# Seven products for w_in: partial sums that accumulate in PSUM, and four additions that also take the row maximum

## The chip, the core and the metric

The kernel runs on one core of a Trainium2 chip. The core has a matrix engine (TensorE, PE in the profile, with its weight loads as PEld), a vector engine (DVE), a scalar engine (ACT), GpSimd (POOL) and a queue engine (SP) that here only issues transfers. Each engine takes its own instructions strictly in the order in which they were written, and engines wait for one another by semaphores. PE's results go to banks of PSUM, which DVE and ACT read; the other tiles lie in SBUF. The metric is the device time of one execution in microseconds, as the median of several runs.

## The reference

```python
q_n, k_n = rmsnorm(q, g_q), rmsnorm(k, g_k)            # q, k, v: (8, 12, 448, 64)
scores = q_n @ k_n.T / sqrt(64)
attn = softmax(scores);  o = attn @ v
x = o.transpose(0, 2, 1, 3).reshape(3584, 768)
h = x @ w_in                                           # (768, 1024)
sm = exp(h - max(h)) / (sum(exp(h - max(h))) + 1e-9)   # along the row
solu = h * sm
ln = (solu - mean) / sqrt(var + 1e-6) * g_ln           # along the row
out = ln @ w_out                                       # (1024, 768)
```

## The kernel before

The work has three stages on PE: attention, the product with `w_in`, and the product with `w_out`. `fast_path` writes them out in one order; a general path behind a flag is not run with these inputs.

**Attention.** Two pairs of heads, `a` and `b`, make one turn `m` of a loop of 24. In a turn DVE transposes the normalised queries and keys of the next turn (`qk_transpose`, L723), adds two of three tiles of exponentials (`add`, L839, tile `es`) and takes sums of squares (`row_sums`, L664, tile `part`); POOL normalises (`normalise`, L713, tile `qkn`) and folds (`fold_sums`, L674); ACT squares, takes exponentials (L802) and applies a gain (L727). PE ends a turn with row sums of the exponentials (`sums`, L884), first of `E`, then of `es` of `a` and of `es` of `b`. The first four turns have places of their own for these steps.

**Product with w_in.** Rows are taken in 14 groups of 256 (two tiles of 128 rows). A group is one 2 by 2 block product in Winograd's form: seven products P1 to P7 of 128x384 by 384x512 take the place of eight. Each product is three matmuls of 128x128 by 128x512 (L982), and the profile shows each matmul as two PE records. With b a block of `w_in`, and a a block of x or a sum of blocks that POOL made (`block_sums`, L962 to L966), the four quarters of the result are c11 = P1+P2, u2 = P1+P6, u3 = u2+P7, c22 = u3+P5, c12 = u2+P5+P3 and c21 = u3+P4. Each product goes to a PSUM bank of its own (`mul`, tags "t" with three buffers and "o" with two). ACT copies P1 out (L993), and DVE makes seven additions per group (`plus`, L989), four into quarters of the row tile `h` and three into `part` tiles in SBUF. When a tile's two quarters are there, `done` schedules its chain: row maximum (`ff_max`, L1036, DVE), exponential (`ff_exp`, L1042, ACT), product (`ff_mult`, L1046, DVE), moments (`ff_moments`, L1054 to L1062, DVE and POOL), scaling (`ff_norm`, L1066, ACT), and a transpose with four stores to memory (`ff_spread`, L1075 and L1078, DVE and SP).

**Product with w_out.** Seven outer products of seven inner products each, for each of seven groups of 512 rows (L1177, 128x128 by 128x192). Here the inner products already accumulate in a bank: bank A takes P1, then P6, then P7, then P4 on top, and each partial sum is read out between (by `plus`: ACT at L1189, DVE at L1191). The operands are read back from memory (`load_u`) and summed by DVE (L1138 to L1144) and POOL (`inner_sums`, L1155 to L1158). Two outer products are interleaved: each starts one at slot 0, 4, 8, 10, 12, 16, 20 of its own and the next begins seven slots later.

**What sets the order.** `unit(f)` writes out one step and advances a clock of four ticks (one tick per slot in the last stage); `later(n, f)` puts a follow-up n units on; `follow(p, i, f)` hangs a follow-up on part i. In the stage of `w_in` a unit is one product. Also hung there are the conversion of `w_out` (three steps per piece: ACT L535 and L536, DVE L541 and L542, ACT L547), 44 combinations of `w_out` blocks on POOL (L563), the loads of x (`load_x`, L934, on ACT's queue from group 2 on) and squares of x (`sizes`, L943, ACT).

## Time and profile before

| what | us |
|---|---|
| median of 5 runs (819.33 to 824.94) | 824.14 |
| the profiled execution, its own time | 824.36 |
| its span | 822.5 |
| attention, to the first matmul of L982 | 332.1 |
| product with w_in, 332.1 to the first matmul of L1177 | 584.6 |
| product with w_out and end | 822.5 |

The profiled execution takes 1.86 us more than its span, and is 0.22 us above the median of the runs. PE is busy for 802.2 us of the span (98%), DVE for 672.3 (82%), ACT for 461.4, POOL for 463.8. A record of a matmul is longer (592 ns) than the distance to the next one, because matmuls are pipelined: from the first to the last of the 588 records of L982 there are 252.0 us, 0.429 us each, so that a product of six records takes 2.575 us. In a timeline the columns are start, length, engine, line, operation, output, input, count, and in brackets the idle time before it with what ended it. In a table of stretches they are the stretch, its length, busy time (with instructions) of PE, PEld, DVE, ACT and POOL, granted clock, DMA share and GB/s.

### The profile page before, as it was taken

Reading aid. Unit: us, or ns where it says so; the run is one execution under the profiler, and the core shown is the slowest. Engines: PE = TensorE matmul, PEld = TensorE weight load, DVE = VectorE, ACT = ScalarE, POOL = GpSimd, SP = SyncE. Lnnn points to the kernel's source line nnn. Section 1 sums busy time; section 2 is a strip of 40 time slices with the busy share of each in tenths; the row PEclk is TensorE's granted clock in tenths of the full one; section 3 lists DMA queues with packets and bytes.
Section 4 is the critical chain, followed back from the end, with each engine's and each line's share of the span. In section 5 each row is a group of like instructions: output and inputs, shape, how many; then the busy total and the mean of one; then the engine's idle time right before and its main releaser. Section 6 shows DMA issues by size and latency. Waiting matters only on the chain.

```text
span 822.5 us, 14941 instructions
## 1 busy us (share of the span) xinstructions
PE 802.2 (98%) x5030; PEld 469.0 (57%) x5030; DVE 672.3 (82%) x1203; ACT 461.4 (56%) x757; POOL 463.8 (56%) x635
## 2 busy tenths in 40 slices
PE   8999999998999999999999999999899999999996
PEld 4333444433334443444444444444689999999996
DVE  6867888887879888589999999998896866866945
ACT  6676778766878777255665544442425464464410
POOL 1334545545555647322254368776487867777861
PEclk9999999999999999999999999999999999999999
DMA  6678778677777663225555534552448356466312
GB/s 132 139 137 203 159 173 197 147 148 175 151 177 173 136 154 120 90 77 152 162 147 141 140 98 117 147 145 63 144 153 273 133 200 233 132 234 209 118 59 82
DMA packets 271938, 122.74 MB, mean 149 GB/s; under 512 B 190444, under 2 KB 257004, under 8 KB 271852
## 3 DMA queue, kind: packets, MB, share of 16 engines
q1 hardware_dynamic: 256668, 111.79, 51.7%
q10 hardware_dynamic: 15184, 9.90, 4.3%
q8 instruction: 42, 0.69, 0.4%
q14 instruction: 44, 0.36, 0.1%
HBM read 84.94 MB, written 36.70 MB: 148 GB/s over the span
## 4 chain that ended last, share of the span: by engine, by line
PE 75%; SPq 10%; DMA 5%; DVE 3%; POOL 3%; issue 2%; ACT 0%; DVEq 0%; POOLq 0%; ACTq 0%
PE b L982 31%; PE A L1177 14%; SPq L634 9%; PE o L865 7%; PE s L812 7%; PE B L1177 7%; DMA v<-in_v_dram 4%; PE C L1177 3%; PE sm L884 3%; PE s L825 1%; PE o L854 1%; DVE part L664 1%; POOL qkn L713 1%; POOL ss L674 1%; DMA qk<-in_q_dram 0%
## 5 line engine op out<-in xcount | busy, mean ns | idle before, releaser
L982 PE MATMUL b<-w_in,xg 128*128 128x512 f32 x336 | 151.1, 592 | 0.0
L802 ACT ACTIVATE E<-s 128x896 f32<-128x896 f32 x168 | 139.0, 933 | 14.2 <-PE s L812 13.9
L812 PE MATMUL s<-qkT 64*64 64x448 f32 x1152 | 121.4, 548 | 2.1 <-ACT qkT L786 1.2
L982 PE MATMUL b<-w_in,xsum 128*128 128x512 f32 x252 | 115.0, 592 | 0.0
L865 PE MATMUL o<-E,v 128*64 128x448 f32 x576 | 113.5, 543 | 0.0
L982 PEld LDWEIGHTS b<-w_in,xg 128*128 128x128 f32 x336 | 63.8, 190 | 80.2 <-issue 77.1
L674 POOL COPY ss<-part 32x56 f32<-32x56 f32 x88 | 42.2, 479 | 96.8 <-DVE part L664 94.1
L713 POOL TENSOR_TENSOR qkn<-qk,ny 128x896 f32<-128x896 f32 x46 | 78.6, 1729 | 29.0 <-DMA qk<-in_k_dram 12.6
L1177 PE MATMUL A<-w_out,sums 128*128 128x192 f32 x392 | 81.1, 330 | 4.0 <-ACT u L1189 2.6
L812 PEld LDWEIGHTS s<-qkT 64*64 64x64 f32 x1152 | 47.3, 163 | 62.0 <-ACT E L802 31.7
L982 PEld LDWEIGHTS b<-w_in,xsum 128*128 128x128 f32 x252 | 47.9, 190 | 60.3 <-issue 57.6
L1060 POOL TENSOR_TENSOR he<-he,mhalf 128x1 f32<-128x1 f32 x28 | 17.1, 609 | 114.3 <-DVE he L1059 112.3
L865 PEld LDWEIGHTS o<-E,v 128*64 128x64 f32 x576 | 39.2, 137 | 72.7 <-issue 64.2
L1177 PE MATMUL B<-w_out,sums 128*128 128x192 f32 x392 | 79.8, 326 | 0.0
L1066 ACT ACTIVATE u<-u,shift,he 128x1024 f32<-128x1024 f32 x28 | 34.7, 1240 | 73.3 <-POOL shift L1062 70.7
L1177 PEld LDWEIGHTS A<-w_out,sums 128*128 128x128 f32 x392 | 67.1, 193 | 5.4 <-issue 2.9
L1177 PEld LDWEIGHTS B<-w_out,sums 128*128 128x128 f32 x392 | 66.2, 190 | 0.2
L664 DVE TENSOR_REDUCE part<-sq 128x28 f32<-128x896 f32 x46 | 48.7, 1078 | 9.8 <-ACT sq L656 8.1
L723 DVE STREAM_TRANSPOSE qkT<-qkn 128x896 f32<-128x896 f32 x46 | 49.0, 1094 | 6.1 <-POOL qkn L713 6.1
L839 DVE TENSOR_TENSOR es<-E 128x896 f32<-128x896 f32 x48 | 53.4, 1114 | 0.5 <-ACT E L802 0.5
L563 POOL TENSOR_TENSOR w_out<-w_out 128x384 f32<-128x384 f32 x44 | 50.7, 1158 | 1.9
L656 ACT ACTIVATE sq<-qk 128x896 f32<-128x896 f32 x46 | 43.7, 982 | 9.4 <-DMA qk<-in_k_dram 8.9
(143 smaller groups left out, 1500.8 us busy)
## 6 DMA issues: line engine op xcount, KB each, us to landing
ur<-ud SPq DMA_DIRECT2D x60, 256.0 KB, 4.8
ud<-ub SPq DMA_DIRECT2D x112, 128.0 KB, 2.3
xd<-xo SPq DMA_DIRECT2D x24, 448.0 KB, 4.2
qk<-in_q_dram SPq DMA_DIRECT2D x184, 56.0 KB, 2.5
qk<-in_k_dram SPq DMA_DIRECT2D x184, 56.0 KB, 2.2
v<-in_v_dram SPq DMA_DIRECT2D x24, 384.0 KB, 4.4
out_dram<-P SPq DMA_DIRECT2D x21, 384.0 KB, 3.6
raw<-in_moe_w_in_dram SPq DMA_DIRECT2D x12, 512.0 KB, 5.1
```

What stands on the lines that cost most here:

```text
L563: nc.gpsimd.tensor_tensor(o, p, q, OP.subtract)
L634: nc.sync.dma_start(d["qk"][g * 32 : g * 32 + 32, s], src[b, h0 + g // 2].rearrange("(b t) (x d) -> x t b d", t=32, x=2)[g % 2],)
L664: nc.vector.tensor_reduce(norms[m]["part"][:, i], st[n]["sq"], AX, OP.add)
L674: e.tensor_copy(ss[g * 32 : g * 32 + 32], part[o * 32 : o * 32 + 32])
L713: e.tensor_tensor(d["qkn"], d["qk"].rearrange("p s b d -> p (s b) d"), y.rearrange("p b -> p b ()").to_broadcast([P, 2 * NB, 32]), OP.mult,)
L723: nc.vector.transpose(d["qkT"].rearrange("p s t -> p (s t)"), d["qkn"].rearrange("p b d -> p (b d)"))
L802: nc.scalar.activation(d["E", kc], s[:, :, 0:S], AF.Exp)
L812: nc.tensor.matmul(s[c : c + D, h, 0:S], d["qkT"][hh, 1, keys], d["qkT"][hh, 0, :], start=True, stop=True,)
L839: nc.vector.tensor_tensor(d["es"], d["E", 0], d["E", 1], OP.add)
L865: nc.tensor.matmul(d["o"][h * D : (h + 1) * D, :], quads[n // 2]["v"][:, n % 2 * 2 + h, kc], d["E", kc][:, h], start=False, stop=(kc == NJ ...
L982: nc.tensor.matmul(o, a[:, c], w_in[i][:, c], start=(c == 0), stop=(c == HD - 1))
L1177: nc.tensor.matmul(k[bank], a[:, c].rearrange("p a i -> p (a i)"), w_out[:, area, i, c], start=begin and c == 0, stop=c == KC - 1, skip_gr ...
```

## The change

In the stage of `w_in`, bank A takes P1, then P6 on top, then P7 on top; after each of the three ACT copies the partial sum out (q1, u2, u3). Bank B takes P5, and later P3 on top. C takes P2, D takes P4. A and C share the three buffers of tag "t", B and D the two of tag "o". Four DVE instructions per group remain (`tensor_tensor_reduce`: bank plus partial sum into a quarter of `h`, and a running row maximum `top`, which the second quarter of a tile takes over from the first); the built program has each of them as two instructions, the second writing `top`. The maximum of a tile is then only negated (128x1), at once.

The order of the products is P6, P5, P7, P1 of the next group, P4, P2 of the next group, P3. The chain of a tile starts at once and its waits become 1, 2, 3, 5 and 7 units for exponential, product, moments, scaling and spread (they were 2, 3, 5, 7 and 10, and in the last group 2, 3, 5, 6 and 8). In attention, the addition `add(a)` of turns 2 and 3 moves from in front of the two transposes of the next turn to behind them, as in later turns.

```diff
-    def products(g, c11, c12, c21, c22, done):
+    def products(g, done):
-        def mul(a, i):
+        def mul(bank, a, i, begin=True):
...
-            tag = "tttoo"[len(banks) % 5]
-            banks.append(tag)
-            o = k["o"] = ps_t.tile([P, 512], FP32, tag=tag, name="b", bufs=3 if tag == "t" else 2)[:, 0:n]
+            if begin:
+                tag = "t" if bank in "AC" else "o"
+                k[bank] = ps_t.tile([P, 512], FP32, tag=tag, name=bank, bufs=3 if tag == "t" else 2)[:, 0:n]
             for c in range(HD):
-                nc.tensor.matmul(o, a[:, c], w_in[i][:, c], start=(c == 0), stop=(c == HD - 1))
+                nc.tensor.matmul(
+                    k[bank], a[:, c], w_in[i][:, c],
+                    start=begin and c == 0, stop=c == HD - 1, skip_group_check=not begin,
+                )
-        def part(name):
+        def part(name, bank):
             k[name] = sums_in.tile([P, 512], FP32, tag="part", name=name, bufs=4)[:, 0:n]
-            return k[name]
-        def plus(out, x):
-            nc.vector.tensor_tensor(out, k["o"], k[x], OP.add)
+            nc.scalar.copy(k[name], k[bank])
+        def plus(row, col, bank, x):
+            t = 2 * g + row
+            d = mt.setdefault(t, {})
+            out = half_of(t, col)
+            top = small.tile([P, 1], FP32, tag="top", name="top")
+            nc.vector.tensor_tensor_reduce(
+                out, k[bank], k[x], 1.0, d.get("top", -3.4e38), OP.add, OP.max, top
+            )
+            d["top"] = top
         def p1():
-            mul("a11", 0)
-            nc.scalar.copy(part("q1"), k["o"])
+            mul("A", "a11", 0)
+            part("q1", "A")
+        def p2():
+            mul("C", "a12", 1)
+            plus(0, 0, "C", "q1")
         def p6():
-            mul("s2", 5)
-            plus(part("u2"), "q1")
+            mul("A", "s2", 5, False)
+            part("u2", "A")
+        def p5():
+            mul("B", "s1", 3)
         def p7():
-            mul("s3", 4)
-            plus(part("u3"), "u2")
-        def p5():
-            mul("s1", 3)
-            plus(c22(), "u3")
-            plus(k["u2"], "u2")
+            mul("A", "s3", 4, False)
+            part("u3", "A")
+            plus(1, 1, "B", "u3")
         def p4():
-            mul("a22", 6)
-            plus(c21(), "u3")
+            mul("D", "a22", 6)
+            plus(1, 0, "D", "u3")
             done(1)
         def p3():
-            mul("s4", 2)
-            plus(c12(), "u2")
+            mul("B", "s4", 2, False)
+            plus(0, 1, "B", "u2")
             done(0)
...
-        nc.vector.tensor_reduce(d["nmax"], d["h"], AX, OP.max, negate=True)
+        nc.vector.tensor_scalar(d["nmax"], d["top"], -1.0, None, OP.mult)
...
-    def in_parts(g):
-        def done(i):
+    def in_parts():
+        def done(g, i):
             t = 2 * g + i
-            waits = (1, 2, 3, 5, 6, 8) if g == NG - 1 else (1, 2, 3, 5, 7, 10)
-            for x, f in zip(waits, (ff_max, ff_exp, ff_mult, ff_moments, ff_norm, ff_spread)):
+            ff_max(t)
+            for x, f in zip(WAITS, (ff_exp, ff_mult, ff_moments, ff_norm, ff_spread)):
                 later(x, lambda f=f: f(t))
...
+        parts = [p[0][1], p[0][2]]
+        for g in range(NG):
+            turn = [p[g][6], p[g][5], p[g][7], p[g][4], p[g][3]]
+            x = len(parts)
+            if g + 1 < NG:
+                turn[3:] = [p[g + 1][1], p[g][4], p[g + 1][2], p[g][3]]
+            parts += turn
+            if g + 1 < NG:
+                follow(parts, x, lambda g=g: sizes(g + 1))
+                follow(parts, x + 1, lambda g=g: block_sums(g + 1, 0))
+                follow(parts, x + 2, lambda g=g: block_sums(g + 1, 1))
+            if g + 2 < NG:
+                follow(parts, x + 4, lambda g=g: load_x(g + 2))
+        return parts
+    WAITS = (1, 2, 3, 5, 7)
...
             unit(lambda: scores(a, 1))
             if m == 2:
                 norms_next()
-            if 1 < m < 4:
-                add(a)
             unit(lambda: scores(a, 2))
...
-            if m > 3:
+            if m > 1:
                 add(a)
             unit(lambda: scores(b, 2))
```

More of the change, by code (lines that the diff above doesn't have):

```diff
@@ L984, in part @@
-        def part(name):
-            k[name] = sums_in.tile([P, 512], FP32, tag="part", name=name, bufs=4)[:, 0:n]
-            return k[name]
-        def plus(out, x):
-            nc.vector.tensor_tensor(out, k["o"], k[x], OP.add)
-        def p1():
-            mul("a11", 0)
-            nc.scalar.copy(part("q1"), k["o"])
-        def p6():
-            mul("s2", 5)
-            plus(part("u2"), "q1")
-        def p2():
-            mul("a12", 1)
-            plus(c11(), "q1")
-        def p7():
-            mul("s3", 4)
-            plus(part("u3"), "u2")
@@ L1015, in p4 @@
             done(1)
         def p3():
-            mul("s4", 2)
-            plus(c12(), "u2")
+            mul("B", "s4", 2, False)
+            plus(0, 1, "B", "u2")
             done(0)
-        return [p1, p6, p2, p7, p5, p4, p3]
+        return {1: p1, 2: p2, 3: p3, 4: p4, 5: p5, 6: p6, 7: p7}
     def half_of(t, i):
@@ L1081, in ff_spread @@
             )
-    def in_parts(g):
-        def done(i):
+    def in_parts():
+        def done(g, i):
             t = 2 * g + i
-            waits = (1, 2, 3, 5, 6, 8) if g == NG - 1 else (1, 2, 3, 5, 7, 10)
-            for x, f in zip(waits, (ff_max, ff_exp, ff_mult, ff_moments, ff_norm, ff_spread)):
+            ff_max(t)
+            for x, f in zip(WAITS, (ff_exp, ff_mult, ff_moments, ff_norm, ff_spread)):
                 later(x, lambda f=f: f(t))
-        h = [lambda t=2 * g + k, i=i: half_of(t, i) for k in range(2) for i in range(2)]
-        p = products(g, *h, done)
-        if g + 2 < NG:
-            follow(p, 6, lambda: load_x(g + 2))
-        if g + 1 < NG:
-            follow(p, 1, lambda: sizes(g + 1))
-            follow(p, 2, lambda: block_sums(g + 1, 0))
-            follow(p, 3, lambda: block_sums(g + 1, 1))
-        return p
+        p = [products(g, lambda i, g=g: done(g, i)) for g in range(NG)]
+        parts = [p[0][1], p[0][2]]
[13 more added lines that the diff above has]
+    WAITS = (1, 2, 3, 5, 7)
     ORDER = ("P1", "P5", "P6", "P2", "P7", "P3", "P4")
@@ L1516, in open_first @@
             last["first"] = pool(ctx, "first", side="right")
-        parts = []
-        for g in range(NG):
-            parts += in_parts(g)
-        n_parts = len(parts)
+        parts = in_parts()
         for x in range(n_in, len(wq)):
```

## The prediction

> **What bounds the kernel now.** I read the page's busy shares first, then a table of stretches, then the groups of the stage that changes, and last the timelines of the places where PE waits.

> ```profile
> PE 802.2 (98%) x5030; PEld 469.0 (57%) x5030; DVE 672.3 (82%) x1203; ACT 461.4 (56%) x757; POOL 463.8 (56%) x635
> ```

> ```profile
> 440.00:480.00 40.00, 40.00 (x95) 17.76 (x94) 39.03 (x62) 21.18 (x33) 18.70 (x24) 1.00 0.41 112
> ...
> 592.00:596.00 4.00, 4.00 (x18) 4.00 (x18) 4.00 (x6) 1.82 (x5) 0.40 (x1) 0.67 0.57 152
> ...
> 584.58:613.23 28.65, 24.43 (x133) 22.81 (x132) 27.86 (x54) 10.84 (x22) 18.32 (x23) 0.94 0.50 147
> 613.23:641.90 28.67, 28.67 (x176) 28.55 (x177) 21.01 (x48) 12.61 (x28) 21.90 (x26) 1.00 0.64 210
> ```

> In the product with w_in (first line) DVE is nearly full, 39.03 of 40 us, but PE is full and sets the time: 588 records at 0.429 us make 252.3 of the stage's 252.5 us. Relief for DVE buys nothing there. It can buy something where the stages meet: from 584.58 to 613.23 PE does 33 inner products, in the steady stretch after it one takes 0.65 us, so 33 x 0.65 = 21.45 and 7.2 us are lost. DVE is busy there for 27.86 of 28.65 us. This timeline shows what ends the losses:

> ```profile
> 589.44 1.15 ACT L1042 ACTIVATE u<-h,hmax 128x1024 f32<-128x1024 f32 x1 [3.69 <-DVE ub L1075]
> ...
> 591.25 1.62 PE L1177 MATMUL A<-w_out,sums 128*128 128x192 f32 x4 [2.61 <-ACT u L1189]
> ...
> 611.34 1.22 DVE L1140 TENSOR_TENSOR s<-s,a 128x512 f32<-128x512 f32 x1
> ...
> 612.74 0.34 DVE L1191 TENSOR_TENSOR u<-A,P 128x192 f32<-128x192 f32 x1
> ...
> 613.23 0.89 PE L1177 MATMUL A<-w_out,sums 128*128 128x192 f32 x4 [0.78 <-POOL sums L1156]
> ```

> First ACT stands at an exponential whose buffer a late spread (ub) frees, and the copies out of bank A wait behind it. The last loss is put down to POOL, but its sums ended before; bank A's partial sum was read at 612.74 to 613.08 by DVE, behind a queue of old chains. DVE's queue has no gap of over 0.7 us from 584.78 to 623.

> **Part 1, the stage of w_in.** The 294 products' matmuls are the same, at 0.429 us a record: 0. DVE, per group, from these rows (busy and mean ns of one):

> ```profile
> L1036 DVE TENSOR_REDUCE hmax<-h 128x1 f32<-128x1024 f32 x26 | 31.7, 1218 | 0.7
> L989 DVE TENSOR_TENSOR h<-b,u 128x512 f32<-128x512 f32 x40 | 27.3, 682 | 4.1 <-PE b L982 4.0
> L993 ACT COPY q<-b 128x512 f32<-128x512 f32 x13 | 7.5, 577 | 8.1 <-PE b L982 8.1
> ```

> Before: 7 additions x 0.68 + 2 maxima x 1.22 = 7.2 us. After: 4 fused rows and 2 negations (0.2 each, as the 128x1 row of L1058). No row of before shows a fused row. At the least it is the addition, 0.68; at the most the parts done singly, 0.68 + half a maximum 0.61 + an accumulator read like ACT's 0.19 = 1.48. I take the addition's pitch and a short second instruction, c = 0.75, since it streams the same 512 columns. So 3.4 us, 3.8 less per group, worth 0 while PE has no gap. ACT gets two more copies, 1.15 us in 18 us; it is busy for 21 of 40.

> [...]

> What can cost is the new waits on PE, which never waits now. Two are tight, each with one product (2.575 us) of slack. (a) The next group's P5 takes B's buffer once the fused row of P3 has read it. From the end of the next P2 to that P5 lie two products, 5.15 us; on DVE lie in order 0.2 to start, c, a spread (1.16 from start to start), a multiplication (1.10; 1.55 on average and up to 1.97 beside POOL), c, and 0.15 to signal: 4.1 at c = 0.75, slack 1.05, or 0.2 beside POOL at its worst. (b) P7 adds onto A once ACT has copied u2, and that copy stands on ACT behind the exponential of the tile just finished: negation 0.2, exponential and its read 1.3, copy 0.6, signal 0.15 after the same fused row; it ends 3.6 us after P3 against 5.15. In the first half a conversion stands in the way: its DVE pair (1.1) between multiplication and fused row in two groups, its ACT pair (1.2) before the copy in two others. Those four go from 1.05 and 1.5 to about 0, and with POOL beside them to -0.5. The other waits (u3's copy for C's buffer, c22's row before P3, q1 before P6) have two or three products. I take +0.4 us, between 0 (all slacks hold) and, at c = 1.48 with the mean multiplication of 1.33, (2.83 + 2 x 1.48 - 5.15) x 13 = 8.3.

> The x loads stay on ACT's queue (0.4 us to issue each) and go out behind the exponential after P4, two products before (b). The spreads' stores, eight transfers per group on SP, come three units earlier, past the w_out loads. Cover: ACT converts a piece some units after its load, and DMA is at 0.41. If it is gone, ACT stands at L535 in front of a copy, as once before at the stage's start for 4.1 us; from 0 to 4.1, taken as 0.

> **Part 2, where the stages meet.** Count from the last product's end (584.6 before). DVE's queue after it loses one maximum (start to start 1.14) and one spread (1.15), which the shorter waits put ahead of the last addition; it gains a negation and a second instruction, 0.4. So 1.9 us lighter. PE's start: both exponentials now stand ahead of the first copy out of A. The last ends at 0.2 + 0.75 + 0.2 + 0.1 + 1.3 = 2.6, the copy at 3.0, so the fourth product starts at 3.1, not 1.95: +1.15. The 2.61 us gap before the seventh goes. But `ff_norm` of tile 27 now stands on ACT ahead of the copy of u3, and it needs moments and POOL: DVE goes maximum, multiplication, two sums s2, spread, moments to 7.2, POOL's two to 8.2, ACT's scaling to 9.4, an operand copy and the u3 copy to 10.2. The tenth product starts there instead of at 7.0: 3.2 more. In before it started at 594.93, 10.35 after the end: nearly the same. POOL's sums of s2 now stand behind both tiles' L1060; they start at 11.9, and their second is done at 13.4, before the sixteenth product at 14.1 (before 14.25).

> The clock: after the gap of 2.61 us the granted clock was 0.67 in one stretch, and three inner products took 1.41, 1.28 and 0.99 instead of 0.65, 1.7 us. After a gap of 0.60 one took 0.75. A gap of 3.2 is nearer to the first, so 1.7 again. [...]

> So PE alone would be 1.15 + 3.2 + 1.7 = 6.05 late, 1.15 better than 7.2, and DVE's late sums by up to 1.9. Both bound the gain at 613; I take 1.0. Ends: 1.9, and -0.5 if norm 27 or POOL come a row later than I placed them.

> **Part 3, attention.** The two moved additions:

> ```profile
> 46.82 1.08 DVE L839 TENSOR_TENSOR es<-E 128x896 f32<-128x896 f32 x1
> 49.50 1.11 DVE L723 STREAM_TRANSPOSE qkT<-qkn 128x896 f32<-128x896 f32 x1 [1.59 <-POOL qkn L713]
> 51.15 1.11 DVE L723 STREAM_TRANSPOSE qkT<-qkn 128x896 f32<-128x896 f32 x1 [0.54 <-POOL qkn L713]
> ...
> 53.15 1.08 DVE L839 TENSOR_TENSOR es<-E 128x896 f32<-128x896 f32 x1
> ```

> ```profile
> 54.28 0.58 PE L884 MATMUL sm<-es,ones 128*32 128x224 f32 x8 [0.96 <-DVE es L839]
> ```

> The first addition now fills an idle stretch; moved behind both transposes it pushes the second, for which PE waits, by 1.0. But POOL's normalisation beside it took 2.38 us (49.42 less 47.04), and 1.68 without (3.36 for two at 72.71). Relieved, the transposes come 0.7 sooner. Net +0.3 in each of two turns, PE is full from 74 to 138, so +0.6. Ends: +2.0 without relief, 0.

> **Sum.** 824.36 + 0.4 - 1.0 + 0.6 = 824.36; the median stands 0.22 lower: 824.1 us.

> **Rivals.** (B) The fused rows or the u2 copies make PE wait in every group. For it: slacks of 1.05 and 1.5 us, and POOL that stretches multiplications; against: DVE's lighter load. It decides from c above 1.16 at the mean multiplication. At 0.35 us in 13 groups, 4.6: 828.7; at c = 1.48, 832. (C) The meeting of the stages empties: DVE is early enough that no wait of the 7.2 us is left. 824.1 + 1.0 - 7.2 = 817.9. For it: the longest gap ends by an early spread; against: DVE keeps four fifths of its queue, and ACT and POOL get new waits. (D) The additions in attention cost their full price, and the stage a little: 824.1 + 1.4 to + 3.5. That DVE's relief does nothing at all is in my forecast, as PE has no gap.

> **Numbers.** About 0.5%, 4.1 us, is what a measurement of this kernel can tell from no change. Forecast 0.48 (821.5 to 826), B 0.28, C 0.14, D 0.10. B lies above 828.3; C below 820: faster 0.14, same 0.58, slower 0.28. The range goes from 819.5, which leaves out most of C, to 830, which leaves out the worse part of B.

> **What would show it.** Right: 0.0 idle in front of L982's matmuls, its records still 252 us in all; a fused row of 0.7 with a second one of about 0.1; DVE at some 32 of 40 us; from the last L982 to the 34th inner product 27 to 28 us; PE's wait for es at about 1.3 us. Wrong: a row "PE A" or "PE B" that waits for ACT u or DVE h in each group, a fused row above 1.2 us, or a meeting of under 24 us.

## The result, and the profile after

The changed kernel takes 824.18 us (median of 36 runs, 820.11 to 826.93) against 824.15 us before (62 runs, 819.33 to 826.77). The ratio is 1.0005 with a 95% interval of 0.9993 to 1.0017, in time -0.6 to +1.4 us. Run once more, beside the kernel before, it gave 1.0015 (0.9999 to 1.0031). So there is no change that a measurement of this kernel can tell, and the forecast of 824.1 us holds. Not all of its steps do.

The two profiled executions differ by more than the medians, 822.5 us of span before and 823.8 after, and can be laid side by side by place. (The profiled execution of the kernel after took 826.1 us, 1.9 above its median. The end of a last product is put where the next record would start without a wait, 0.16 us before the end of its own last record.) The last column is the second profile of the kernel after, 822.5 us of span:

| stretch | before | after | difference | predicted | after, once more |
|---|---|---|---|---|---|
| start to the first matmul with w_in | 332.13 | 332.07 | -0.06 | +0.6 | 331.26 |
| stage of w_in, to the end of its last product | 252.45 | 252.88 | +0.43 | +0.4 | 252.46 |
| from there to the start of the 34th inner product ("the meeting") | 28.65 | 30.08 | +1.43 | -1.0 | 29.93 |
| rest | 209.27 | 208.77 | -0.50 | 0 | 208.85 |

The longer meeting is there in both profiles of the kernel after, the longer stage of w_in in one.

First the busy shares of the changed kernel (busy us, share of the span, instructions).

```profile
PE 801.8 (97%) x5030; PEld 469.9 (57%) x5030; DVE 617.7 (75%) x1217; ACT 475.1 (58%) x785; POOL 469.1 (57%) x635
```

DVE lost 54.6 us of work and PE's 801.8 us stayed. The table of stretches says where (length; busy us of PE, PEld, DVE, ACT, POOL; granted clock; DMA share and GB/s). The first line lies in the stage of w_in, the second is the meeting, the third the steady stretch behind it.

```profile
440.00:480.00 40.00, 40.00 (x95) 17.75 (x94) 29.07 (x64) 23.39 (x39) 21.79 (x25) 1.00 0.50 128
584.95:615.03 30.08, 25.05 (x133) 24.47 (x133) 24.27 (x54) 10.08 (x20) 18.23 (x24) 0.89 0.65 193
615.03:643.70 28.67, 28.67 (x177) 28.55 (x177) 21.00 (x48) 12.75 (x28) 20.77 (x25) 1.00 0.63 210
```

In the stage of w_in DVE falls from 39.03 to 29.07 of 40 us and PE stays full: relief for an engine that PE does not wait for. In the meeting DVE also has 3.6 us less to do than before (27.86), yet the meeting got longer and its clock lower (0.89, before 0.94).

The groups of the changed operations show the price of the fused row (busy, mean ns of one, idle time before them and what ended it).

```profile
L998 DVE CUSTOM_DVE_ANT_0 h<-D,u,top 128x512 f32<-128x512 f32 x14 | 10.4, 743 | 25.3 <-PE D L982 25.3
L998 DVE CUSTOM_DVE_ANT_0 h<-C,q 128x512 f32<-128x512 f32 x14 | 9.7, 692 | 18.7 <-PE C L982 16.7 <-ACT tmp L535 2.0
L998 DVE DVE_READ_ACCUMULATOR2_ANT top<- 128x1 f32 x56 | 4.6, 82 | 0.0
L1047 DVE TENSOR_SCALAR hmax<-top 128x1 f32<-128x1 f32 x28 | 4.3, 154 | 1.0
L982 PE MATMUL B<-w_in,xsum 128*128 128x512 f32 x168 | 76.7, 592 | 0.0
L982 PE MATMUL A<-w_in,xg 128*128 128x512 f32 x168 | 74.7, 593 | 0.2 <-ACT u L989 0.2
```

A row costs 0.69 us, or 0.74 with the running maximum as an operand, and a read of 0.08; predicted were 0.7 and 0.1. The last two lines are PE's: in 588 records it was idle 0.2 us.

The meeting is best read on PE's timeline of the changed kernel (start, duration, operation; in brackets the idle time and its releaser).

```profile
585.97 0.92 PE L1194 MATMUL A<-w_out,a 128*128 128x192 f32 x4 [0.85 <-DVE top L998]
...
591.27 0.81 PE L1194 MATMUL A<-w_out,sums 128*128 128x192 f32 x4
596.26 1.65 PE L1194 MATMUL A<-w_out,a 128*128 128x192 f32 x4 [4.18 <-ACT u L1206]
597.70 1.49 PE L1194 MATMUL B<-w_out,sums 128*128 128x192 f32 x4
598.98 1.49 PE L1194 MATMUL C<-w_out,s 128*128 128x192 f32 x4
...
602.66 0.81 PE L1194 MATMUL A<-w_out,a 128*128 128x192 f32 x4
```

Three losses stand there. The first inner product starts 1.02 us after the last product's end (584.95), because its PSUM bank is the one in which the last group's B waits for its fused row. The tenth product waits 4.18 us for ACT's copy of u3 and starts 11.3 us after the end. Behind it the products take 1.1 to 1.4 us instead of 0.65: from the tenth to the seventeenth 7.70 us instead of 4.55, 3.15 us of slow clock. After that PE waits for nothing.

ACT's timeline shows what the copy of u3 (the last line) stood behind:

```profile
588.87 0.32 ACT L1206 COPY u<-A 128x192 f32<-128x192 f32 x1 [0.33 <-PE A L1194]
593.72 0.62 ACT L1151 COPY a<-ur 128x512 f32<-128x512 f32 x1 [4.53 <-DMA ur<-ud]
594.25 1.24 ACT L1077 ACTIVATE u<-u,shift,he 128x1024 f32<-128x1024 f32 x1
595.39 0.60 ACT L1151 COPY a<-ur 128x512 f32<-128x512 f32 x1
595.90 0.31 ACT L1206 COPY u<-A 128x192 f32<-128x192 f32 x1
```

Two things are late at once. The operand copy (L1151) waits until 593.72 for its load, and the scaling of tile 27 (`ff_norm`, L1077), which could not start before 593.70 either, is next. Why the load is late shows on SP's queue, first of the changed kernel, then of the kernel before (start of issue, time in the queue, transfers):

```profile
584.82 1.83 SPq L1089 DMA_DIRECT2D ud<-ub  x4
586.76 2.82 SPq L1131 DMA_DIRECT2D ur<-ud  x6
```

```profile
575.80 2.79 SPq L1114 DMA_DIRECT2D ur<-ud  x6
```

With a delay of 7 units instead of 10 the spread of tile 25 is written ahead of the six loads of the stage of w_out (`load_u`). The four stores go out at 584.82, when DVE's transpose of 583.55 to 584.80 is done, and the loads stand behind them: they go out at 586.76, 11 us later than before.

### The profile page after: what moved, and what is told of

Read it like the earlier page. It is cut to its first block, busy times and chain, and to the rows that moved or that the text cites. A ratio compares the mean times of both kernels' runs of the same rounds, so it can differ in the third digit from the quotient of the medians.

```text
span 823.8 us, 14988 instructions
## 1 busy us (share of the span) xinstructions
PE 801.8 (97%) x5030; PEld 469.9 (57%) x5030; DVE 617.7 (75%) x1217; ACT 475.1 (58%) x785; POOL 469.1 (57%) x635
## 4 chain that ended last, share of the span: by engine, by line
PE 74%; SPq 11%; DMA 4%; DVE 4%; issue 3%; POOL 2%; ACT 1%; ACTq 0%; DVEq 0%; POOLq 0%
PE A L1194 15%; PE A L982 12%; SPq L634 9%; PE B L1194 8%; PE s L812 7%; PE o L865 7%; PE B L982 7%; PE D L982 4%; PE C L982 4%; PE C L1194 4%; PE sm L884 3%; DMA v<-in_v_dram 1%; PE s L825 1%; PE o L854 1%; DVE part L664 1%
## 5 line engine op out<-in xcount | busy, mean ns | idle before, releaser
L713 POOL TENSOR_TENSOR qkn<-qk,ny 128x896 f32<-128x896 f32 x46 | 77.1, 1696 | 28.4 <-DMA qk<-in_k_dram 12.0
L1071 POOL TENSOR_TENSOR he<-he,mhalf 128x1 f32<-128x1 f32 x28 | 28.2, 1006 | 106.8 <-DVE he L1070 106.3
L812 PEld LDWEIGHTS s<-qkT 64*64 64x64 f32 x1152 | 47.3, 163 | 61.4 <-ACT E L802 31.7
L982 PE MATMUL B<-w_in,xsum 128*128 128x512 f32 x168 | 76.7, 592 | 0.0
L982 PE MATMUL A<-w_in,xg 128*128 128x512 f32 x168 | 74.7, 593 | 0.2 <-ACT u L989 0.2
L1053 ACT ACTIVATE u<-h,hmax 128x1024 f32<-128x1024 f32 x28 | 32.2, 1148 | 64.3 <-DVE hmax L1047 64.3
L982 PEld LDWEIGHTS A<-w_in,xg 128*128 128x128 f32 x168 | 31.8, 190 | 40.6 <-issue 39.1
L982 PEld LDWEIGHTS B<-w_in,xsum 128*128 128x128 f32 x168 | 31.9, 190 | 40.2 <-issue 38.5
L723 DVE STREAM_TRANSPOSE qkT<-qkn 128x896 f32<-128x896 f32 x46 | 48.9, 1093 | 6.6 <-POOL qkn L713 6.6
L839 DVE TENSOR_TENSOR es<-E 128x896 f32<-128x896 f32 x48 | 53.3, 1112 | 0.5 <-ACT E L802 0.5
L563 POOL TENSOR_TENSOR w_out<-w_out 128x384 f32<-128x384 f32 x44 | 45.1, 1031 | 1.3
```

Of the source, the lines that this page charges most:

```text
L563: nc.gpsimd.tensor_tensor(o, p, q, OP.subtract)
L713: e.tensor_tensor(d["qkn"], d["qk"].rearrange("p s b d -> p (s b) d"), y.rearrange("p b -> p b ()").to_broadcast([P, 2 * NB, 32]), OP.mult,)
L723: nc.vector.transpose(d["qkT"].rearrange("p s t -> p (s t)"), d["qkn"].rearrange("p b d -> p (b d)"))
L812: nc.tensor.matmul(s[c : c + D, h, 0:S], d["qkT"][hh, 1, keys], d["qkT"][hh, 0, :], start=True, stop=True,)
L839: nc.vector.tensor_tensor(d["es"], d["E", 0], d["E", 1], OP.add)
L982: nc.tensor.matmul(k[bank], a[:, c], w_in[i][:, c], start=begin and c == 0, stop=c == HD - 1, skip_group_check=not begin,)
```

## Experiments on the meeting of the stages

All edits are made on the changed kernel unless said otherwise. In every run I take, from the end of the last product with w_in, the start of the tenth and of the 34th inner product. "Extra, 10 to 17" is the time from the tenth to the seventeenth product beyond 4.55 us, where the tenth had waited. Before is 10.35 and 28.65, after 11.31 and 30.08. The run "attention put back" has the meeting of the kernel after unchanged (its edit is described further down), so the first three rows show how far one kernel scatters: 0.4 us at the tenth and 1.0 at the 34th. The four runs below them were executed once each (822.01, 824.60, 823.18 and 821.26 us, the kernel before beside them 821.16), too few to compare the whole; only their stretches are used.

| run | tenth at | its wait | extra, 10 to 17 | 34th at |
|---|---|---|---|---|
| after | 11.31 | 4.18 | 3.15 | 30.08 |
| after, once more | 11.54 | 4.41 | 2.78 | 29.93 |
| attention put back | 11.73 | 4.60 | 1.49 | 29.10 |
| other bank | 10.79 | 3.82 | 1.78 | 28.61 |
| stores behind the loads | 10.79 | 3.66 | 1.78 | 28.61 |
| scaling later | 10.31 | 3.19 | 3.10 | 29.15 |
| both moves | 6.97 | 0 | - | 26.97 |

**The bank.** The first bank of the new pool is given to another tag.

```diff
         last["ps"] = pool(ctx, "ps_o", space=bass.MemoryType.PSUM)
+        last["ps"].tile([P, 512], FP32, tag="B1", name="B")
```

> The first PSUM bank of the w_out stage is made another one than that which the last group's partial sum B lies in. In the kernel after the change the first inner product waited 1.02 us there, and the 34th started 30.08 us after the last product with w_in. Theory, order on ACT: the tenth product waits for the copy of u3, whose place on ACT is set by the row statistics of tile 27 and by loads, not by PE, so the first products start 1.0 us earlier, the tenth wait grows by 1.0 to about 5.2 us, and the 34th stays at 30.1 (29.6 to 30.6). Rival, the waits add up: the 34th comes at 29.1 or earlier.

The first wait is gone, but the fourth product then waited 0.72 us for ACT's copy of q, so the ninth came only 0.16 us sooner, and the wait of the tenth remained:

```profile
585.14 0.89 PE L1194 MATMUL A<-w_out,sums 128*128 128x192 f32 x4 [0.72 <-ACT q L1206]
593.11 0.92 PE L1194 MATMUL A<-w_out,a 128*128 128x192 f32 x4 [3.82 <-ACT u L1206]
```

In its reason the theory held: time won ahead of the tenth is swallowed there. Its numbers did not: the tenth's wait fell to 3.82 us where 5.2 was expected, and the 34th came 1.47 us sooner, at 28.61, which meets the rival's number (29.1 or earlier). Of that, 0.52 lies before the tenth (ACT's operand copy got its load 8.15 us after the end, before the edit 8.77), and 1.37 in a shorter stretch of slow clock; the stretch behind the seventeenth took 0.42 back. By the trace none of this is the bank's wait itself, and the slow clock varies as much without an edit (1.49 to 3.15 in the first three rows).

**The stores of tile 25 behind the loads.**

```diff
+        if t == NT - 3:
+            later(2, store)      # store(): the loop of four stores
+        else:
+            store()
```

> Only the four stores of tile 25's spread are moved behind the six loads of the stage of w_out on SP. The loads then go out some 11 us sooner (about 576 instead of 586.8). Theory, both orders matter: the copies of a12 on ACT no longer wait for DMA, but the scaling of tile 27, ahead of the copy of u3, still waits for POOL's shift at 593.7; the tenth product comes only 0.5 us sooner (10.8 after the last product with w_in instead of 11.3), and the 34th 0.5 sooner, 29.6. Rival, the late loads alone made the loss: the tenth product is not late, and the 34th comes at 23 to 26.

ACT now has its operand in time and stands at the scaling, for POOL's shift:

```profile
589.01 0.62 ACT L1158 COPY a<-ur 128x512 f32<-128x512 f32 x1
593.65 1.24 ACT L1077 ACTIVATE u<-u,shift,he 128x1024 f32<-128x1024 f32 x1 [4.02 <-POOL shift L1073]
```

The tenth came at 10.79, as expected (10.8); the 34th 1.0 us better than expected, again by the shorter slow clock. The rival falls: late loads alone did not make the loss.

**The scaling of tile 27 later.**

```diff
+            waits = (1, 2, 3, 6, 7) if t == NT - 1 else WAITS
```

> Only the scaling of tile 27 on ACT is moved behind the copies of u3 and of the next product's u2. Theory, both orders matter: the first copy of a12 still waits for its load until 593.7, a second one follows, and the copy of u3 comes out at 595.1 instead of 596.2; the tenth product is 1.1 sooner (10.2 after the last product with w_in) and the 34th 1.0 to 1.5 sooner, 28.6 to 29.1. Rival, the scaling alone made the loss: the 34th comes at 23 to 26.

Now the load is what ACT waits for. The tenth came at 10.31 (expected 10.2), the 34th at 29.15 (expected 28.6 to 29.1).

```profile
591.70 1.26 ACT L1152 COPY a<-ur 128x512 f32<-128x512 f32 x2 [4.55 <-DMA ur<-ud]
592.87 0.31 ACT L1207 COPY u<-A 128x192 f32<-128x192 f32 x1
```

**Both moves.**

> Both moves together. Theory 1, the order on ACT and SP is all that was lost: the tenth product starts without a wait (about 7 us after the last product with w_in), neither the gap of 4.2 us nor the slow clock behind it (3.2 us) is left, and the 34th product starts at 22.7. Theory 2, what the prediction called DVE decides below: the next waits stand close behind, the fourteenth product for DVE's row out of bank B (queued until 596.6), the sixteenth for POOL's sums of s2 behind the second power (598.9 by the profile); a gap of about 3 us comes with part of the clock loss, and the 34th starts at 26 to 27.5.

Each move alone made the tenth 0.5 and 1.0 us sooner; together 4.3, ten times the scatter of the tenth. That is what two causes side by side look like. PE's waits with both moves are now these:

```profile
594.71 0.92 PE L1202 MATMUL B<-w_out,sums 128*128 128x192 f32 x4 [2.00 <-DVE P L1246]
596.97 0.92 PE L1202 MATMUL A<-w_out,sums 128*128 128x192 f32 x4 [0.69 <-POOL sums L1181]
598.96 0.92 PE L1202 MATMUL B<-w_out,sums 128*128 128x192 f32 x4 [0.42 <-DVE P L1254]
609.95 0.89 PE L1202 MATMUL A<-w_out,sums 128*128 128x192 f32 x4 [0.33 <-POOL sums L1180]
```

Theory 2 takes up the bound that the prediction sets at 613, where it has DVE's sums late by up to 1.9 us. The 34th at 26.97 lies in its range (26 to 27.5), and the two waits came where it had put them, at the fourteenth product for DVE and at the sixteenth for POOL. The clock stayed at full speed after the 2.00 us.

The last of the four lines, the 34th product, is not POOL's although the trace names it. The product reads the third of POOL's sums of s3, which was done at 604.12; the sum that the trace names is one of a22, for later products. The product also needs bank A read out by DVE, and that ended at 609.80, 0.15 us ahead of it. In the kernel before and in every run here where PE waits in front of the 34th product, it starts 0.14 to 0.15 us after this read, and its own sum was done over 5 us earlier. So "DVE decides below" is true of the kernel with both moves, beside POOL, and not of the kernel after.

**DVE's rows first.** Both moves and the other bank, and the chain of tile 26 later:

```diff
+            if g == NG - 1:
+                waits = (1, 2, 3, 6, 7) if i else (1, 3, 5, 6.25, 7.5)
```

> Both moves of the run before (stores of tile 25 behind the six loads; the scaling of tile 27 later) and the other bank, and on DVE the multiplication and the moments of tile 26 are put behind the rows that empty banks C and B of the first outer product (scaling and spread of tile 26 later by as much). Theory 2 (DVE's queue comes next): the fourteenth product finds bank B read at about 9.9 us after the last product with w_in instead of 11.7; a gap of 1.4 us is left, the clock stays, POOL's sums of s2 stand ahead of the second power, and the 34th product starts at 23.5 to 24.5 where it was 30.1 in the kernel after and 27.0 with the two moves. The whole then takes 5.5 to 6.5 us less than the kernel after: 817.5 to 819. Rival, POOL takes the place of DVE (its sums pushed by the late power): the 34th stays at 26.5 to 27.5 and the whole at 820.5 to 821.5.

The fourteenth product came at 9.8 after a wait of 0.20 us, as theory 2 said. But the 34th stayed at 27.37, since a wait on ACT came up behind:

```profile
596.13 0.62 ACT L1159 COPY a<-ur 128x512 f32<-128x512 f32 x1 [1.79 <-DMA ur<-ud]
596.65 0.31 ACT L1216 COPY u<-A 128x192 f32<-128x192 f32 x1
```

```profile
597.02 0.92 PE L1204 MATMUL A<-w_out,s 128*128 128x192 f32 x4 [1.40 <-ACT u L1216]
598.81 1.35 PE L1204 MATMUL B<-w_out,sums 128*128 128x192 f32 x4 [0.87 <-DVE P L1256]
```

The copy for the next 512 rows (a11) waits for its load ahead of the copy of u3. The rival's number was met, but by ACT and not by POOL; neither theory had this wait. The whole: 822.94 us (expected 817.5 to 819) against 825.53 of the kernel before on that chip, ratio 0.9975 (0.9954 to 0.9996).

**The next three waits, one after another.** In the first run the a11 copies of the next 512 rows come two slots later on ACT, and the spread of tile 27 later on DVE. In the second, moments, scaling and spread of tile 26 are put further behind. In the third, the first run is taken again and POOL's sums of s2 are put ahead of tile 27's power, into the time in which POOL stood idle.

```diff
-            made(n, "a11", base + 12 + late, base + 15 + late)
+            more = 2 if n == 1 else 0
+            made(n, "a11", base + 12 + late + more, base + 15 + late + more)
...
+                waits = (1, 2, 3, 6, 8.25) if i else (1, 3, 5, 6.25, 7.5)     # first
+                waits = (1, 2, 3, 6, 8.25) if i else (1, 3, 6.5, 7.5, 8.5)    # second
+                waits = (1, 2, 3.5, 6, 8.25) if i else (1, 3, 5, 6.25, 7.5)   # third
...
+                    slot = 4 if (n, q) == (0, 2) else STEP * q - 6            # third
```

> The reordered kernel, with two more moves: the copies of the next super tile's a11 on ACT, the first of which waited for its load at 596.1 ahead of a copy of u3, come two slots later, and the spread of tile 27 on DVE behind the row that empties bank B at 598.4. There PE had waited 1.40 and 0.87 us, and after them four products ran at half clock, about 1.9 us. Theory (each wait stands directly behind the one removed, and DVE's queue is the last): the seventeenth product starts without a wait, the eighteenth waits up to 1.1 us for DVE, the clock stays, and the 34th product starts at 23.5 to 25 after the last product with w_in, where it was 27.2. Rival, another wait of the same length follows: 26.5 or later.

> As the run before, and the moments, scaling and spread of tile 26 come behind the last rows of the first two outer products. Theory: DVE then keeps up with PE, no wait over 0.5 us is left among the first 33 inner products, and the 34th starts at 22 to 23.5 after the last product with w_in, 6.5 to 8 us before that of the kernel after; the whole takes 817 to 818.5 where the kernel before takes 824.15, 0.6 to 0.9% less. Rival, DVE's 2.1 us of moments only stall a later product: the 34th at 24 to 26, the whole 819.5 to 821.5.

> The kernel before the last one (reordered, a11 copies later, spread of tile 27 later), and POOL's four sums of s2 are put ahead of the power of tile 27, four slots sooner; the moments of tile 27 come a little later. POOL stood idle until 589.2 and then worked without a gap until 609, and the 34th product waited 1.37 us for its sums. Theory (POOL's queue is the last wait): the s2 sums fall into the idle stretch, the chain on POOL is 2 to 3 us sooner, the 34th product no longer waits and starts at 24.0 to 25.0 after the last product with w_in instead of 25.8; the whole takes 3 to 5 us less than the kernel before on the same chip. Rival, the sums beside DVE's work stretch both and the power of tile 27 comes later: the 34th stays at 25.5 to 26.5, the whole 2 to 3 us below the kernel before.

| run | waits of PE before the 34th | 34th at | whole against before |
|---|---|---|---|
| first | 0.72 ACT, 0.20 and 0.92 DVE, 1.37 DVE at the 34th | 25.93 | one run, 819.26 |
| second | 0.72 ACT, 0.20 and 1.50 DVE, 0.79 DVE at the 34th | 25.90 | 0.9974 (0.9960 to 0.9989) |
| third | 0.72 ACT, 0.45 and 0.76 DVE, 0.78 DVE at the 34th | 25.43 | 0.9971 (0.9956 to 0.9986) |

All three stayed behind their theories (23.5 to 25, 22 to 23.5, 24 to 25), nearer to the rivals: each removed wait left another. In the second, DVE's deferred moments stalled a later product by 1.50 us, as its rival had it. In the third the wait of the 34th fell to 0.78 us, no lower than in the second, where POOL's sums had not moved:

```profile
594.56 0.92 PE L1204 MATMUL B<-w_out,sums 128*128 128x192 f32 x4 [0.45 <-DVE P L1248]
598.18 0.92 PE L1204 MATMUL B<-w_out,sums 128*128 128x192 f32 x4 [0.76 <-DVE P L1256]
609.97 0.89 PE L1204 MATMUL A<-w_out,sums 128*128 128x192 f32 x4 [0.78 <-POOL sums L1182]
```

The two candidates for the last of these waits, POOL's sum that this product reads and DVE's read of bank A:

```profile
602.96 1.18 POOL L1184 TENSOR_TENSOR sums<-s 128x256 f32<-128x256 f32 x1
609.48 0.34 DVE L1218 TENSOR_TENSOR u<-A,P 128x192 f32<-128x192 f32 x1
```

The expectation of the third run took the 1.37 us for POOL's, by the name in the trace. They were DVE's, so the run moved sums for which the 34th product did not wait; what its 0.5 us came from was not separated, since its moments of tile 27 on DVE also moved.

The third has the lowest ratio of the versions timed against the kernel before: 821.76 us, with 823.79 before and 825.00 for the kernel after on the same chip. The intervals of the three reordered versions that were timed in this way overlap, so none is shown to be better than the others. Its ratio of 0.9971 is about 2.4 us less than before; its meeting is 3.2 us shorter than that of before and 4.65 shorter than that of after.

## Experiments on the other two parts

**The maximum alone.** In the kernel before, only the four last additions of a group take the maximum along.

```diff
-            plus(c11(), "q1")
+            total(0, c11(), "q1")     # tensor_tensor_reduce(out, k["o"], k[x], 1.0, top, OP.add, OP.max, top)
```

> The kernel before with one part of the change alone: its last additions take the row maximum along, and the two maxima over a whole tile become negations. Products, partial sums in SBUF, order and waits stay as before. DVE loses two maxima (2 x 1.22) and gains four accumulator reads (4 x 0.08), two negations (2 x 0.15) and up to 4 x 0.07 a group: about 1.6 us of 18 lighter, from 39.0 to about 35.5 of 40 us. Theory (DVE is not the bound in this stage): the stage stays at 252.5 us, and only the meeting of the stages can move, by at most 1 us each way: 823.2 to 824.5. Rival, DVE at 98% was a hidden bound: the stage gets shorter and the whole takes 2 us less or better.

```profile
440.00:480.00 40.00, 40.00 (x94) 17.67 (x93) 35.76 (x73) 22.17 (x36) 20.32 (x25) 1.00 0.50 134
```

DVE fell to 35.76 of 40 us (expected 35.5), and from the first matmul with w_in to the start of the last product's record lie 249.87 us, to the hundredth as before. The whole: 824.09 us, ratio 0.9986 (0.9971 to 1.0002). DVE at 98% was not a hidden bound of this stage. The meeting, with DVE lighter there too, was 28.35 us long (before 28.65).

**The fused row taken apart.**

```diff
-            nc.vector.tensor_tensor_reduce(
-                out, k[bank], k[x], 1.0, d.get("top", -3.4e38), OP.add, OP.max, top
-            )
+            nc.vector.tensor_tensor(out, k[bank], k[x], OP.add)
+            nc.vector.tensor_reduce(top, out, AX, OP.max)
+            if "top" in d:
+                nc.vector.tensor_tensor(top, top, d["top"], OP.max)
```

> The kernel after with the fused row taken apart: an addition, a maximum over its 512 columns, and for the second half of a tile a maximum of two columns. The price of a finished half, c in the prediction, goes from 0.8 to about 1.4 to 1.6 us. Theory (the chain on DVE between P3 and the next P5 has 1.05 us of slack, in 13 groups, and two prices lie in it): PE waits for DVE in nearly every group, 0.4 to 0.8 us each, and the stage gets 5 to 10 us longer, 258 to 263 us; the whole 829 to 834. Rival, PE's order has more slack than was counted: the stage stays within 1 us of 252.9.

The stage got 11.0 us longer, 263.87 us, and the whole 1.9% (840.06 us, ratio 1.0191, 1.0154 to 1.0229, above the 829 to 834 expected; the profiled run, 835.2 us, is the fastest of its four, and what the others lost on top was not looked at). All of PE's waits in the stage:

```profile
397.16 5.39 PE L982 MATMUL A<-w_in,xg 128*128 128x512 f32 x12 [2.71 <-issue]
416.44 5.39 PE L982 MATMUL A<-w_in,xg 128*128 128x512 f32 x12 [1.02 <-ACT u L989]
456.16 7.08 PE L982 MATMUL A<-w_in,xg 128*128 128x512 f32 x12 [3.27 <-ACT u L989]
512.91 5.39 PE L982 MATMUL A<-w_in,xg 128*128 128x512 f32 x12 [0.32 <-ACT u L989]
531.53 5.39 PE L982 MATMUL A<-w_in,xg 128*128 128x512 f32 x12 [0.36 <-issue]
```

The size is near what was expected, the place is not. Not every group pays, and P5 never waits for B: the addition alone frees the bank, and the maximum behind it does not count, which the expectation had overlooked. With it the chain in front of P5 is 2.83 + 1.5 + 0.7 = 5.0 of 5.15 us. What gives way is P7, which waits for the copy of u2, in five groups, 7.7 us together (for two of them the trace names no releaser, "issue", at the same product); of the remaining 3.3, 1.7 are slow clock (7.08 instead of 5.39 us behind the longest wait, the only slow stretch of this stage), and the rest lies in records that start 0.1 to 0.2 us late around these waits and at P7 of other groups. At 456 ACT's copy stood behind the exponential, which waited for the maximum, behind DVE's conversion rows. So slack (b) of the prediction is the tight one, and the three longest waits lie in groups with a conversion, as it said; the two of 0.32 and 0.36 us come after the last conversion (468.3). Rival B's own condition, c above 1.16 in front of P5, was not put to the test.

**The additions in attention put back.**

```diff
+            if 1 < m < 4:
+                add(a)
             unit(lambda: scores(a, 2))
...
-            if m > 1:
+            if m > 3:
                 add(a)
```

> Only the two additions of attention are put back behind the scores in turns 2 and 3, where they stood before. Theory (the cost is real in its place and is taken up later by DMA): PE's waits for es fall from 1.23 to about 0.96 us in turn 2 and vanish in turn 3, turn 4 starts 0.3 to 0.5 us sooner, and at the first product with w_in (332.1) and in the whole nothing is left of it: 823.7 to 824.6. Rival, as the prediction's sum has it: the 0.5 us stay to the end, 823.6; a second rival, the additions at their old place now cost more because the order around them differs: later than 824.6.

PE's waits for `es` in the kernel after, and in this one:

```profile
54.33 0.58 PE L884 MATMUL sm<-es,ones 128*32 128x224 f32 x8 [1.23 <-DVE es L839]
...
69.00 0.59 PE L884 MATMUL sm<-es,ones 128*32 128x224 f32 x8 [0.24 <-DVE es L839]
```

```profile
54.17 0.59 PE L884 MATMUL sm<-es,ones 128*32 128x224 f32 x8 [0.96 <-DVE es L839]
68.05 1.12 PE L884 MATMUL sm<-es,ones 128*32 128x224 f32 x16
```

The local cost is shown, 0.27 and 0.24 us. What becomes of it is not: the whole gave 1.0002 (0.9978 to 1.0026), and the first matmul with w_in starts anywhere from 329.6 to 332.4 us in the runs that share the attention of the kernel after. Half a microsecond cannot be followed through that.

## Why the prediction was right, and where it was not

**Part 1, right in reason, in size within what one execution tells.** +0.4 predicted, +0.43 measured in this profile. From the first to the last of the 588 records lie 252.44 us in it, in the ten other profiles with the same stage 252.02 to 252.95, in five of these as much as before to 0.01 (252.02). c is 0.77 to 0.82 with its read, and where PE waits it is at one place: a P7 at 414.92, 0.18 us idle and 0.35 late, in a group with a conversion (idle there 0.64 and 0.69 us in the two longest stages). That is slack (b), as the prediction had it. Its terms for (b) add up to 3.2 us, not 3.6, which does not matter here. DVE came to 29 of 40 us where it said 32. The fused row took 0.69 us, or 0.74 with the running maximum as an operand, against 0.68 for the plain addition before.

**Part 2, wrong.** The predicted gain of 1.0 us was a loss of 1.43 (1.28 and 0.45 in two more profiles of this meeting), and the steps that failed are these.
- DVE as the bound at 613 ("Both bound the gain"; DVE decides below, as theory 2 has it). In the kernel before it was: the last wait ended with DVE's read of bank A, as the prediction read it. DVE's queue was indeed lighter, but in the kernel after PE waits for DVE nowhere behind the tenth product. Both-moves shows what this bound would have needed: with ACT's and SP's waits gone, DVE and POOL came next.
- "past the w_out loads ... taken as 0". The prediction counted the stores as moved past the loads of `w_out` pieces. It missed that the earlier spread of tile 25 also passes the six loads of the next stage, with a wait of its own in front of them. The stores themselves cost nothing; what was queued behind them did. Alone it was worth 0.5 us at the tenth product, together with the scaling 4.3.
- The tenth product: `ff_norm` of tile 27 in front of the copy of u3 was seen, and 10.2 us predicted; 11.3 came, for the power took 1.39 instead of 0.55 us and the late load pushed a second copy behind the scaling.
- The clock: 1.7 us taken from the length of the gap; 3.15 lost, and 2.78 and 1.49 in the other two profiles. The loss does not go by the length alone (last section).
- The first bank of the next stage is the last group's B: not seen. It costs 1.02 us in its place and, by the trace, nothing at the tenth. So the fourth product came at 3.07 us, where 3.1 was predicted, by luck: not ACT's copy but the bank held it; with the other bank the copy did, at 2.83.

**Part 3, right in place.** +0.3 in each turn predicted, +0.26 and +0.27 measured. The two profiles then meet again at 332 us (from 170 to 250 us both have gaps in PE, at a DMA share of 0.70 to 0.76), so nothing of it reached the end there; whether it is taken up in general stays open.

**The sum** came within 0.1 us of the measured median by luck. Laid side by side, the two profiles differ by 1.3 us where 0 was predicted: part 2 is 2.4 us off, part 3's 0.6 and the 0.5 of the rest go the other way. What is no luck is that every one of these errors is small against the 4.1 us that a measurement can tell. Rival C (the meeting empties, 817.9) was further off than it looked: seven moves got from 30.1 to 25.4 us, not to 21.5, as behind each wait the next engine's stood close.

## What to carry to other kernels

When a delay is shortened, list for each in-order queue, SP's included, what the step now stands in front of; here the four stores themselves cost nothing, and the wait that they brought along put six loads 11 us later. Check the releaser that a trace names against the operand that is read: at the 34th product of both moves the trace named a sum for a later product, where DVE's read of the bank ended 0.15 us ahead of it. If two waits end at nearly the same time, removing one can show a fraction of their worth (here 0.5 and 1.0 of 4.3 us), so try both together before either is written off. Freeing an engine on which the bottleneck did not wait bought nothing here, even at 98% busy (ratio 0.9986, 0.9971 to 1.0002), but the same relief may decide whether a tighter chain still fits (here the copy of u2: with the row taken apart PE waited 7.7 us for it).

## What the runs showed of the hardware

```profile
592.25:595.66 3.41, 0.00 (x0) 0.00 (x0) 3.24 (x9) 1.94 (x3) 1.36 (x3) 1.00 0.99 300
595.66:599.07 3.41, 2.81 (x9) 2.81 (x10) 1.84 (x5) 3.41 (x8) 3.23 (x5) 0.50 0.46 175
599.07:602.49 3.42, 3.42 (x12) 3.42 (x11) 0.71 (x3) 0.96 (x3) 3.34 (x6) 0.50 0.71 218
```

```profile
593.88:597.29 3.41, 2.85 (x9) 2.85 (x10) 1.67 (x4) 3.41 (x8) 3.23 (x6) 0.50 0.67 219
597.29:600.70 3.41, 3.41 (x23) 3.41 (x22) 1.98 (x4) 1.05 (x3) 3.33 (x6) 1.00 0.47 170
```

So in these runs a gap counted by how it lay in the steps. The 2.61 us before lay almost whole in one (2.56), and the 1.40 and 0.87 us of DVE's rows first fell into one together (2.15); the 2.00 us of both moves were divided between two, with 0.60 and, part of the next gap included, 1.85 us, and there the clock stayed at 1.00 through the whole meeting. The loss was about half of the slow time in which PE was not idle: (6.83 - 0.60) / 2 = 3.1 us in the kernel after, where 3.15 was lost, and (3.41 - 0.56) / 2 = 1.4 with attention put back, where it was 1.49. The code of the meeting is the same in both; the first slow step began 0.60 us ahead of the tenth product in the one and 0.56 us ahead in the other.

POOL's power of 128x1 values took 0.55 us at the least in the kernel after, and 1.39 to 1.48 where it started at most 0.24 us after DVE's product of two SBUF tiles, as here in the meeting (timelines of DVE and of POOL):

```profile
591.71 1.22 DVE L1057 TENSOR_TENSOR u<-h,u 128x1024 f32<-128x1024 f32 x1
```

```profile
591.95 1.39 POOL L1071 TENSOR_TENSOR he<-he,mhalf 128x1 f32<-128x1 f32 x1 [10.32 <-DVE he L1070]
```

Between 332 and 455 us four of the twelve powers of the kernel after started at most 0.2 us after such a product and took 1.46 to 1.48 us, and the others 0.55 to 0.94; in the kernel before none started within one there, and all 28 took 0.54 to 0.95. The mean of all 28 went from 609 to 1006 ns.
